# K and Q stored in DRAM by 512 tokens, a planner that counts eight DMAs in flight, and x1 normalised on VectorE and transposed in row halves

## The chip, the cores and the metric

The kernel runs on one core of one Trainium2 chip. The metric is the device time of one execution in microseconds (us); lower is better. A difference of 0.3% (5.6 us) is about what a measurement of this kernel can tell from no change.

## What is computed

Two blocks read the same normalised input and are added to it: attention with 32 heads of 20 columns, and a mixer of shifted tokens with an MLP behind it. S = 2048 tokens, D = 640, F = 1536, everything float32.

```python
xn = layernorm(x)
# A: attention
q, k, v = split(xn @ wqkv)                 # 32 heads, Dh = 20
o = softmax(q k^T * Dh**-0.5) v
A = o @ wo
# B: mixer; it normalises xn once more
h  = gelu(layernorm(xn) @ w1)
hs = shift(h)  # four groups of 160 columns, shifted by +1, -1, +2, -2 tokens
x1 = xn + hs @ w2
B  = x1 + gelu(layernorm(x1) @ w3) @ w4
out = x + A + B
```

## The kernel before, in words

**Work and tiles.** TensorE (PE) has three kinds of products. *Row pairs*: two matmuls with 64 or fewer rows each lie in the two row halves of the array and run at the same time. All dense products are row pairs (every operand is split into a high and a low part, three products each; `twins`, L737), and so are the attention's two products per step: `s` (scores, keys on the partitions, for the exponential on ScalarE, ACT) and `pm` (scores once more, queries on the partitions, from which VectorE, DVE, takes row maxima `mx` for a later block). *Column groups*: four products with 32 columns each, for `pv` (probabilities by values). *Full products*: 128 by 128, the transposes. `SWITCH` (L79) tells the planner that a change of kind costs time.

The attention is a chain of 1024 units in 32 blocks (a block is a pair of heads and 1024 queries). The dense work is spread among the units as filling: the V, Q and K products, w1, the x1 stage (w2), w3, w4; the output product (wo) follows the attention. One stage matters below, the x1 stage (`w23_phase`, L1085): it comes in two halves of four pairs of 128-token tiles, each half followed by the w3 products. For pair q, `x1_pair` (L1121) makes `ps2` on PE, adds the input on DVE (x1), takes bn_stats and a reciprocal root (`rsqrt`, L672: one power on GpSimd, called POOL, and small steps on DVE), and normalises both tiles of 640 columns in place (L1141 to 1143): planned for POOL at 900 ns each, with a way out to DVE at 430 ns. `z_pair` (L1146) then transposes the two tiles on PE (`tz`, ten full 128 by 128 transposes in three PSUM tiles) and `split_held` (L706) moves each PSUM tile out: a copy on ACT, the low part by a subtraction on DVE.

**What sets the order.** Nothing is issued as the program text stands. All operations go into a planner (`Plan.schedule`, L398), which runs a list schedule with a cost for each and writes the instructions of each engine in the order that comes out. On PE a string of some 7,000 letters, `ORDER` (L98), says at each step which kind of group is next (d dense, m maxima, s scores, p values). The hardware runs each engine's instructions strictly in that order: one that waits holds up all behind it on its engine.

**DMAs in the planner.** All DMAs are issued from SyncE (SP), in planned order. Each costs SP 465 ns; its transfer takes nbytes / 260 ns on one common bus; its data are taken to be there 1500 ns later, plus an allowance `late` by kind: `SLOW` 4500 (weights and dense loads), `PREP` 6500 (raw weight chunks `ph_*`, split and written back as `wd_*` for later), `LATE` 7000 (the chain that ends a block), 0 for Q, K and V of the attention.

**The chain that ends a block** (`block_end`, L1478): the sums in `ob` go to DRAM (`od`), come back as `sm` on 128 partitions, DVE takes the reciprocal `rc`, which goes to DRAM (`rcd`) and comes back broadcast as `rb`; POOL multiplies, and the result goes to `onm`. Four DMAs, one after the other, 30 times.

**K and Q.** They lie in DRAM as `[128, 2, 2048]` (row, high or low part, token), L659 and 660; the products write 512 tokens of both parts at a time, the attention reads rows of one part: 2048 tokens of K, 1024 of Q.

Of the kernel before, what the change touches and what calls it, by code (L numbers as in the profile page):

```python
# [52 lines left out]
XB = 12  # L53
BOOT = 740.0
SLOW = 4500.0
PREP = 6500.0
# [31 lines left out]
LATE = 7000.0  # L88
# [15 lines left out]
    "dsdddsdssddsdsddmdmppppsdddsdssdsddsddsddsdddsdssddddsddsdspssdppsddsdsddddssdpsddsdddsddsdsddssddsddddsddsssd"
    "dsppssdddsppsdsdsdssdsddsdspssspppsdsdsdsddssddsddsddsdsdddssddddssdsddsdddssppsdsdddsdspsspsssppsdsdddsddsdpp"
    "dddssdddsdddssdddddsdddsdsddddsdddddsdddssdddddssddddssdddsddddddssdddddsdppppssdddddssddddddsddddsssddddsdddd"
    "dsdsddsddsdppppsddsdsdddddsdsddddsddssddsddddsdsddddsdsdddspssspppsddsdddsddsdddsdsddddssdddddssdddddssddddsds"
    "ppppdsdsdsddsdddsddddsddddssddsdddsddddddddsdsdddddddssddddsdddddssppppsdddssdsdddsddddsddddddsdddsdddsddsdddd"
    "dsssddddsdddsddsddddsppppddsddsddssdsdddsdsddsddddsssdddsdddssddddssdddsddsppppssddsddsddsdsddsddssddsdsddppss"
    "ddddsdsdddsdsddsdsddsdsdpssspppssddddsdsddsdsppssddsddsdddsssdddsdddssdddssddsdsdddsspssspppsdsdddsddddsdsdsdd"  # L110
    "sdddssdsdddssppppsdsdsdsdddsdsdsdsdddsddddssdsdddsddspppdsddsdsddspssddsddsdsddsdsdsddsdsddssdsppppdsdsdsdddds"
    "dssddsdsddddssdddsdssdddddsddsdsdddssppppsddsdsdsddssdddsdsdsdddsdssddsdsddsdsdpssdddsddsdddssppsddsdsdpppsddd"
    "sdsddsddsdsdddssdddsdsdddsddspdsddssdddsssdppppsdsddddsdddsspssdddsdsdsddssdddsdsdsdddssddspssppsspsdsdssdddss"
    "dppssddddddsdsdddsdsddddssdddsdsdddsdsdddsddsddsppsdddssddddsdssddddsdsdsdsppppdsdsdsddsddsddssdddssddddsdsddd"
    "sdssddsppppdssddsdddsddssddsddsdsdsdsdddsdsddssddspsspsdsdddddssppddsddsddsdsddssdsddssppppsdssddsddsddsdsdsdd"
    "ssddppssddddsdspdssdddsdsddsdsddsdspsddsdsddsdssddddsdssddsddddsddsppppssddsdsdsdddsddsddssddsddsdsdsdsddsddds"
    "dddpsddsddspppdsdsddssdsdddddssdsspsdsppsspsdsdsdsddsdddsdsdsddsddsdddsddsdsddsdsppppddsdddssddsddddssdsddsdsd"
    "ddsdssdddssppsssppssddddddssddddddsdsddssdddsddssddsdsddsdsdddsdsppppsdsddssddsddsdsdsddsdsddsdspsspppssdddssd"
    "dsdddsdsdsdsdddsddsddsdddsdsdsdspdpppsddssddddsssdddsddsddsddssddsddspssddpppdsdsddsddssdsddddssddddssdsdddssd"
    "dsddsddddssddsdpsspppsddsdddddsdsddsdddssddssdsddsddsdspsspsdsdddsdsdddsdspsspssspssspssspssspdssspssspssspsds"  # L120
    "psdsddsddsddddsdddsddssdddddddssddddddsddddddssddddddsddsdppppsddssdddsdsdddddsddsdddddddsddddddddsddddssdddsd"
    "dddddsddddsddsppppdddddddddddddddsddddsddddddssddddsddddddddsdddssppddsddsdddsddsdddddsdspdsddddsdddsddddssddd"
    "dsddddddddddppdsddsddddsddsddddsddsdsddsdddsddsppssdddddsdddddddsdddsdddddddsspssdddddsdsdddsdsdsddddssppssspp"
    "ssdddsdsddddsddddsddsdsdsddsdsddddddsdsddsddssddssdppddsspsdddspsssddddddddddddssppssdsssppsssdddsddddddsddddd"
    "dsssddddsddddsssdddddddddddssddddsddsdsdsdsddpppppsddsdddsddsdddsdsdddddsdddsddddsdddsdsdddssdddddsdddddssdddd"
    "dsddddsddsddpppddsdsddddssdddsdsddssdddssddsdddssdppppsdsddssdddssddsdsddsdsddsdsppppdssdddssddsddsdsdsddsdsds"
    "ddspppssddddsdsdddsdddsdsdddssdddsddsddsdddsdsddddssppppssddddddsdddddsdddsdspsdsdsdsdddsdsdsdsddsdsdddsspsssp"
    "ppsdsddsdsdsdsddddssddsdddssddsdsdddssppppdssdddsdsdsdddsddsddsdddsddssdsdddssddsdsppppssddsdsddsddsdsdsddsdds"
    "ddddsdsddddsddssddddsddpppdsdddsddsddsddsddsdsddspsddssdddsdsdsdsddsdsddsddsppssppsdsddsdsdsdsddddssdsddddsspp"
    "ppdsddsddssdddsdsddsdddddsssddddsdsddsdddssdsddddssppssppsssssspssspssspssspsddsddssdddsdddddsdddssddddsddsdsd"  # L130
    "ddsdddsddsppppsdsddddsdddsddsdddddssddsddsddddsdsddsdddddddsdsddspspppdssdddsddsddddssddddsdsddddsddsddddsdddd"
    "ddddddsddddddsdddsddsddddsddddddsdsddddddsddppppsddssdddddsdsddddddsdssddddsddddssdddsdddsdsddddddddddpppsdsdd"
    "dddsddsddddsdddsdsddsdddsdddsddsdddddddsdddddsdspppppsdddssdddssdddddssddddsdsddsdddddddpsdsddddsdddsddsdddddd"
    "ssdddddsdddsddsdddsddspssddddddsspsspsssppssspssspsssspssddddsddddddspssspssspssssspssspssddddsddddsdddsddddss"
    "dddsdddddsdsddddsdddddddddsdsdddsdddsdpppdddsdddddsddddsdsdddddddddsddsdddddddssdddsddddddssddddddsdpppddddddd"
    "dddddddsssdddsdddsddssddsddsdddssppppdsdsdsdddssdsdddsddsdddsssdddsddsdsddsdsdddssdddsppsssppssdddsdsddsdsddss"
    "ddsdsddsdspppssdddsdsddsdsddsddsddsddsppppdsddsdddddsdddsdsdddsdspssdddssddsdsddsdsddsdsddsdsppppssddsddsdddsd"
    "sdsddsddsddssdsddsdsddsdddsdsdsdddsdsppppssdddsdsddsdsddsdsdsdsddsdsppsdsdddsdsdddsdsddsdsdddsdddddssdppppdsdd"
    "ddsdsdddsdsppssdddsdsdsdsdddssddsdddssddddsddsdddsdssddsddsddsppppsdsddsddsdsdsddsdsdsdddsdddsdsddsdsppppsdsds"
    "ddsddssdddssddsddsdsddsddssdddsddsdspsssppsspsssspsdpssspsddsddddspsdsdddssddddsddsddddsdddsdsdddsddsddsdddsds"  # L140
    "dppppsdsdddddsdddddsdddddsddsddddddsssddddddddddddddsddsddsdddsddddddsdddsddssdddddsdddddsddddsddppppsdsddddsd"
    "sdddsddddsddddsdddsdddssdddsdsdddsddsddddsppppdsdddssdddsdddsdsddsddddddsdddddsddsdddsdsdddddsdsppdppsdsdddsdd"
    "sddddssdddsddddssdddsddsddddsddsddsddddsddsppppsddsddsdddsddddsdddssdsdddddsdddsdsddsdddsdddddssddppppdsdsddds"
    "sddddsddddsddssddddddsdsdddsdsddsddddsdddssdppppdsddssddsddddsddsddsddsdddddsdddsddssdddddsddsddddssppppdssddd"
    "dssdddddsdddsdsdsddddsdddsdddsddsddsddsddsddsddppppsdsddddssdddsdddsddsddddsddsdddsdsddsddsddddsddsdsddppppsds"
    "dddddsddsdsdddsdsddsdddsddddsddsdsddddsddsdddsddsppppssdddddssdddsdsdddsddsddddsdddsddddsdsdddsdddsddddssdpppp"
    "sdsddsdddsdddsddsddsddsdddsdsdddddsdsddsdddsddsdddsdsppppssddddssddddsdsddddsdsdddddsdddsddssddddsdsdddsddddss"
    "ppppsddsddsddsddsdsdddsdddddsddsdddssdddsddddssdddsdddsdsppppsddsdsddddsddssddddsdddsddddsdsddsddddssppppdsdss"
    "ddddddddsssddddddsdddssdddddsdddddssdsddddddsdsddsdddsdsdddsppppssddddddssddsddddsdsddddsddsddsddddsdddddsddsd"
    "dddssppppsddsdsdsddddsdddsdddsdddsdsdddsddsdddsddsddsddsddddssppppsddsdsddddssdddddssdddsdddsdddddsddsdsdsdddp"  # L150
    "pppsdddsddddsssddddddsdddssdddddsdsddddddsdddsddsdsdddsdsdddsddsppppssdddsdsddddsddddsdsdsddddsddsdddsdddsddds"
    "dsddsddddssppppsddsddsddsdsdddsdddddsddsddddssddddssdddsdddsdddddssppppsdddsdsdddsddddsdddssdddsdddsdddsdsdddd"
    "dssppppdsdsddddddsssdddddsdddsdsdddsddddddssddddsdsddsddddsdsddsdddsdppppssddddsdddsdsdsdddddsddsdddsdddsdsddd"
    "sdsddsdddsddsddsppppsdddsdsddsddddsddsddsdsdddddsddssddddddssddsddddddssppppdsdsddsddddsdsddddsddssdddsddddsds"
    "dddddsspdpppdssdddddddsssddddddddsdssddddsddddssddddddsdsdsddsdddsdddddsdsppppssddddsddsdddsdsddsddddsdddsddsd"
# [118 lines left out]
class Plan:  # L274
# [123 lines left out]
    def schedule(self):  # L398
# [1198 lines left out]
```

## Time and profile before

| what | value |
|---|---|
| median of 3 runs | 1866.05 us (1861.46 to 1866.73) |
| the profiled execution's own time | 1867.61 us |
| its span, first to last instruction | 1865.7 us |
| PE, DVE, ACT, POOL busy | 1844.3, 1510.3, 1380.1, 478.0 us |
| mean granted TensorE clock | 0.995 |
| bytes moved by DMA | 257.79 MB |

The profile counts an engine as busy while any of its instructions runs. Matmuls overlap (the next one starts before the last has drained), so a busy PE may still have lost time between two starts; that is read from the starts in the timeline. PEld is the loading of weights. Of an instruction's idle time the tables name what ended it.

### The profile page before, as it was taken

To read this page: it belongs to the slowest core of one execution; us is meant where nothing else is said; L and a number is where in the kernel's file an instruction comes from. 1 tells how busy PE (TensorE), PEld (TensorE's weight loads), DVE (VectorE), ACT (ScalarE), POOL (GpSimd) and SP (SyncE) were. 2 spreads that over 40 slices of the span, in tenths; PEclk is the share of its full clock that TensorE was granted. 3 is DMA by queue.
4 is the path that set the end of the run, shared out by engine and by line. 5 is a ranking of instruction groups with operands and counts; after the bars stand their busy time and mean duration, and the time that the engine had idled before them with its cause. 6 is when DMAs were issued, how large, how long until landed. Compare 5 with 4: busy or idle time off the path is not lost.

```text
span 1865.7 us, 44172 instructions
## 1 busy us (share of the span) xinstructions
PE 1844.3 (99%) x17073; PEld 1277.5 (68%) x17073; DVE 1510.3 (81%) x2678; ACT 1380.1 (74%) x2528; POOL 478.0 (26%) x684
## 2 busy tenths in 40 slices
PE   9999999999999999999999999999999999999998
PEld 7876776666666656576666756665777777775687
DVE  8988788898988898877879997778788778788624
ACT  5268778887888886677887676878777777778762
POOL 6011113423413224412113421111211222212211
PEclk9999999999999999999999999999999999999999
DMA  5644646445464575545335574455524243243503
GB/s 196 169 132 152 154 105 175 134 130 171 120 154 126 159 225 152 165 135 168 111 114 181 179 205 143 140 156 176 132 74 108 85 108 93 69 140 97 168 17 114
DMA packets 230361, 257.79 MB, mean 138 GB/s; under 512 B 60520, under 2 KB 175672, under 8 KB 228352
## 3 DMA queue, kind: packets, MB, share of 16 engines
q1 hardware_dynamic: 230152, 254.98, 46.9%
q8 instruction: 134, 2.20, 0.5%
q14 instruction: 75, 0.61, 0.1%
HBM read 151.64 MB, written 103.25 MB: 137 GB/s over the span
## 4 chain that ended last, share of the span: by engine, by line
PE 92%; DVE 3%; POOL 2%; DMA 2%; ACT 1%; issue 0%; DVEq 0%; SPq 0%; POOLq 0%; ACTq 0%
PE ps L355 26%; PE pv L355 24%; PE s L355 14%; PE pm L355 13%; PE psv L355 4%; PE pso L355 3%; PE ps_q L355 3%; PE ps_k L355 3%; DVE mx L323 2%; PE psl L355 1%; POOL x L323 1%; PE tz L323 1%; DMA kpack<-kd 0%; DMA ph_wo<-in_A_wo_dram 0%; PE pmt L355 0%
## 5 line engine op out<-in xcount | busy, mean ns | idle before, releaser
L323 DVE TENSOR_REDUCE mx<-pm 128x1 f32<-128x512 f32 x2048 | 1272.9, 682 | 207.2 <-PE pm L355 128.8
L323 ACT ACTIVATE p<-s 128x512 f32<-128x512 f32 x2048 | 1104.1, 605 | 205.7 <-PE s L355 79.9
L355 PE MATMUL s<-zq,kpack 62*128 62x512 f32 x2048 | 753.7, 408 | 3.5 <-DVE mx L323 3.2
L355 PE MATMUL pm<-kpack,zq 60*128 60x512 f32 x2048 | 752.9, 408 | 0.8 <-DVE mT L323 0.3
L355 PE MATMUL pv<-p,v 128*32 128x512 f32 x4096 | 488.1, 600 | 0.1
L355 PEld LDWEIGHTS s<-zq,kpack 62*128 62x128 f32 x2048 | 360.7, 185 | 109.9 <-issue 33.4
L355 PEld LDWEIGHTS pm<-kpack,zq 60*128 60x128 f32 x2048 | 361.9, 185 | 97.6 <-DVE mx L323 25.6
L355 PE MATMUL ps<-xT,w_w 64*128 64x512 f32 x2040 | 327.5, 393 | 0.1
L355 PEld LDWEIGHTS pv<-p,v 128*32 128x32 f32 x4096 | 116.9, 109 | 236.6 <-issue 209.2
L355 PEld LDWEIGHTS ps<-xT,w_w 64*128 64x128 f32 x2040 | 210.3, 186 | 36.5 <-issue 6.3
L323 POOL TENSOR_TENSOR ob<-ob,obq 128x512 f32<-128x512 f32 x96 | 124.0, 1292 | 365.7 <-ACT obq L323 321.0
L355 PE MATMUL ps<-xT 64*128 64x320 f32 x1632 | 170.8, 308 | 0.0
L355 PEld LDWEIGHTS ps<-xT 64*128 64x128 f32 x1632 | 146.1, 186 | 15.1 <-issue 5.0
L323 ACT COPY obq<-pv 128x512 f32<-128x512 f32 x84 | 49.3, 587 | 123.5 <-PE pv L355 123.5
L355 PE MATMUL ps<-xT,gT 64*128 64x320 f32 x1152 | 122.2, 306 | 0.0
L343 POOL MEMSET scratch<- 1x1 f32 x134 | 12.2, 91 | 404.8 <-PE ps L355 235.5
L355 PEld LDWEIGHTS ps<-xT,gT 64*128 64x128 f32 x1152 | 105.8, 186 | 6.9 <-issue 0.8
L355 PE MATMUL psv<-wv,xT 64*128 64x320 f32 x960 | 93.1, 309 | 1.1 <-ACT xT L323 1.1
L355 PEld LDWEIGHTS psv<-wv,xT 64*128 64x128 f32 x960 | 81.6, 185 | 8.1 <-issue 2.2
L355 PE MATMUL ps_q<-xT,w_q 64*128 64x512 f32 x480 | 81.8, 395 | 0.2 <-POOL scratch L343 0.2
L355 PE MATMUL ps_k<-xT,w_k 64*128 64x512 f32 x480 | 78.0, 398 | 0.0
L355 PE MATMUL pso<-wos,oT 64*128 64x320 f32 x768 | 67.2, 307 | 0.0
(184 smaller groups left out, 1411.3 us busy)
## 6 DMA issues: line engine op xcount, KB each, us to landing
zq<-qd SPq DMA_DIRECT2D x156, 80.0 KB
kpack<-kd SPq DMA_DIRECT2D x78, 160.0 KB
w_w<-wd_w SPq DMA_DIRECT2D x48, 256.0 KB
gd<-pre SPq DMA_DIRECT2D x8, 1536.0 KB
g<-gd SPq DMA_DIRECT2D x64, 192.0 KB
wd_w<-ph_w SPq DMA_DIRECT2D x34, 320.0 KB
xT<-wd_w SPq DMA_DIRECT2D x34, 320.0 KB
vd<-vst SPq DMA_DIRECT2D x32, 256.0 KB
```

The lines of the kernel that those rows point to most:

```text
L323: o.insts = [getattr(e, m)(val(out), *[val(x) for x in ins], **{k: val(v) for k, v in kw.items()})]
L343: o.insts = [nc.gpsimd.memset(scratch.get(), 0.0)]
L355: o.insts = [nc.tensor.matmul(out.get(), lhsT.get(), rhs.get(), **kw) for out, lhsT, rhs, kw in products]
```

## The change

- `qd` and `kd` become `[128, 4, 2, 512]`: 512 tokens of both parts lie together. A product writes one run of 4096 bytes per row in place of two of 2048; the attention reads runs of 2048 bytes (four per row of K, two of Q) in place of one of 8192 and one of 4096.
- The planner's DMA: SP's cost, and a transfer time worked out from the number of runs and their length over 16 engines; at most eight DMAs in flight; data after 1600 ns plus an allowance that is now 2500 (`SLOW`), 3000 (`PREP`), 3000 (`LATE`), and 1500 for Q and K.
- x1 is normalised on DVE alone.
- `tz` is made of 64-row halves: each 128 by 128 transpose becomes a row pair of two transposes, one per half of the tokens, into two PSUM tiles of up to 512 columns; per pair of tiles there are two rounds (four column tiles, then one), so four PSUM tiles and four copies and subtractions in place of three.
- Two DVE costs in the planner are raised (455 for the addition of 320 columns), and `ORDER` is another string.

```diff
+LANES = 8
-SLOW = 4500.0
-PREP = 6500.0
+SLOW = 2500.0
+PREP = 3000.0
-LATE = 7000.0
+LATE = 3000.0
 ORDER = (
-    "dddddddddddddmddddmdddddddddddddddddddddddddddddmdmdddddddddddddddddddmddddddmddddmdddddddddddddddddddmddddd"
...
+        lanes = [0.0] * LANES
...
             if e == "dma":
                 xbus = max(xbus, o.end) + o.xfer
-                o.end = xbus + 1500.0 + o.late
-                free[e] = max(free[e], xbus - BACKLOG)
+                lanes.append(xbus + 1600.0)
+                o.end = xbus + 1600.0 + o.late
+                free[e] = max(free[e], lanes[-LANES] + 70.0)
...
-    def dma(o, i, nbytes, **kw):
-        op_ = pl("dma", 465.0, "dma_start", o, i, xfer=nbytes / 260.0, **kw)
+    def dma(o, i, nbytes, es=2560, **kw):
+        n = nbytes / es
+        op_ = pl("dma", 375.0 + 100.0 * (n >= 128) + 130.0 * (n >= 256), "dma_start", o, i,
+                 xfer=1.1 * (8.0 + 0.0375 * es) * math.ceil(n / 16), **kw)
...
-    qd = [dt([P, 2, S], F32R, f"qd{c}") for c in range(ND)]
-    kd = [dt([P, 2, S], F32R, f"kd{c}") for c in range(ND)]
+    qd = [dt([P, 4, 2, 512], F32R, f"qd{c}") for c in range(ND)]
+    kd = [dt([P, 4, 2, 512], F32R, f"kd{c}") for c in range(ND)]
...
-                kept[nm, tb] = dma(_f(dst[:, :, tb * 512:(tb + 1) * 512]), _f(hl), 524288)
+                kept[nm, tb] = dma(_f(dst[:, tb]), _f(hl), 524288, 4096)
...
                 for j in range(2):
-                    pl("pool", 900.0, "tensor_scalar", x1[:, j, :], x1[:, j, :], mv[:, j, 0:1], rs[:, j:j + 1],
-                       op0=ALU.subtract, op1=ALU.mult, port=True, alt=("dve", 430.0, "tensor_scalar", True))
+                    pl("dve", 430.0, "tensor_scalar", x1[:, j, :], x1[:, j, :], mv[:, j, 0:1], rs[:, j:j + 1],
+                       op0=ALU.subtract, op1=ALU.mult, port=True)
...
-                for d0 in (0, 2, 4):
-                    n = min(2, ND - d0)
-                    ps = pd(f"tz{q}_{d0}")
+                for d0, n in ((0, 4), (4, 1)):
+                    pss = [pd(f"tz{q}_{d0}_{h}")[:, :P * n] for h in range(2)]
                     for e in range(n):
                         for j in range(2):
-                            transpose(ps[:, e * 256 + j * P:e * 256 + (j + 1) * P], x1[:, j, (d0 + e) * P:(d0 + e + 1) * P])
-                    split_held(xT[:, 0, d0:d0 + n, t0:t0 + 256], xT[:, 1, d0:d0 + n, t0:t0 + 256],
-                             ps[:, :256 * n].rearrange("p (d t) -> p d t", d=n), 256 * n)
+                            c = e * P + j * 64
+                            pl.group("row", 110.0, [(pss[h][:, c:c + 64], x1[64 * h:64 * h + 64, j, (d0 + e) * P:(d0 + e + 1) * P],
+                                                     ident[64 * h:64 * h + 64, 64 * h:64 * h + 64], dict(is_transpose=True))
+                                                    for h in range(2)])
+                            tick(110.0)
...
     def rdma(o, i, nbytes):
-        adma(o, i, nbytes)
+        adma(o, i, nbytes, 1500.0)
```

**PE, before, at the second pair of x1 tiles** (`tz` of the pair with x1 tile 1; `x_1` is the normalised tile, `ps_4` the sums of the next pair):

```order
5508 L355 MATMUL ps_4_1_11831<-xT 128x320
5509 L355 MATMUL ps_4_0_11830<-xT 128x320
5510 L355 MATMUL pm_0_12017<-kpack_76,zq_79 128x512
5511 L355 MATMUL s_1_12018<-zq_80,kpack_77 128x512
5512 L323 MATMUL tz_0_12025<-ident,x_1_11124 128x128 x4
5513 L323 MATMUL tz_2_12032<-ident,x_1_11124 128x128 x4
5514 L323 MATMUL tz_4_12040<-ident,x_1_11124 128x128 x2
5515 L355 MATMUL pv_2_11811<-p_0_11650,v_8708 32x512
```

The ten transposes stand in one piece, between row pairs and a column group. After the change the same pair's transposes begin like this:

```order
5610 L356 MATMUL ps_5_1_12178<-xT 128x320
5611 L356 MATMUL ps_5_0_12177<-xT 128x320
5612 L356 MATMUL s_0_12329<-zq_80,kpack_77 128x512
5613 L356 MATMUL pm_1_12330<-kpack_76,zq_79 128x512
5614 L356 MATMUL pm_0_12333<-kpack_76,zq_79 128x512
5615 L356 MATMUL s_1_12334<-zq_80,kpack_77 128x512
5616 L356 MATMUL tz_0_0_12341<-ident,x_1_11219 128x64
5617 L356 MATMUL tz_0_1_12342<-ident,x_1_11219 128x64
5618 L356 MATMUL tz_0_0_12341<-ident,x_1_11219 128x64
```

They are row pairs among row pairs, and they have moved back behind sums of the pair after next (`ps_5`, where `ps_4` stood).

**DVE, after, at the fourth pair** (`x1_3`), from the addition of its last sums (`ps2_7`) to its normalisation; `mx13` are the attention's maxima, `xT` the low parts of the pair before:

```order
1213 L324 TENSOR_REDUCE mx13_11025<-pm443_1_12831 128x1
1214 L324 SCALAR_TENSOR_TENSOR rv_c3_12097<-mv3_3_12141 128x2
1215 L324 TENSOR_TENSOR xT_201<-tz2_0_1_12823,xT_201 128x4x2x64
1216 L324 TENSOR_REDUCE mx13_11025<-pm443_0_12844 128x1
1217 L324 SCALAR_TENSOR_TENSOR rt_c3_12113<-ry_c3_12142 128x2
1218 L324 TENSOR_REDUCE mx13_11025<-pm444_1_12881 128x1
1219 L324 SCALAR_TENSOR_TENSOR rt_c3_12113<-rt_c3_12113,rv_c3_12097 128x2
1220 L324 TENSOR_TENSOR xT_201<-tz2_4_0_12892,xT_201 128x2x64
1221 L324 SCALAR_TENSOR_TENSOR ry_c3_12142<-rt_c3_12113,ry_c3_12142 128x2
1222 L324 TENSOR_REDUCE mx13_11025<-pm444_0_12900 128x1
1223 L324 TENSOR_TENSOR xT_201<-tz2_4_1_12893,xT_201 128x2x64
1224 L324 TENSOR_SCALAR x1_3_12394<-x1_3_12394,mv3_3_12141,ry_c3_12142 128x640 x2
```

The two normalisations (row 1224) are now in DVE's own line; ahead of these rows stand the two additions, one maximum, two bn_stats, a subtraction and bn_aggr (rows 1207 to 1212).

**SP, the start of a block's closing chain, before** (block 11: `od` out, `sm` back; `rd`, `xr`, `ph` and `xT` are loads and stores of the dense work):

```order
490 L323 DMA od_123<-ob11_11158 4x512
491 L323 DMA rd_117<-xr5_12060 128x640
492 L323 DMA ph_w3_9_1_12311<-in_B_w3_dram 128x2x128
493 L323 DMA xT_201<-hsd2_114 128x2x256
494 L323 DMA xT_201<-hsd3_115 128x2x256
495 L323 DMA xT_201<-hsd4_116 128x2x256
496 L323 DMA rd_117<-xr6_12212 128x640
497 L323 DMA xr7_12526<-in_A_x_dram 128x640
498 L323 DMA sm11_10738<-od_123 128x16
```

And after:

```order
531 L324 DMA od_123<-ob11_11058 4x512
532 L324 DMA wd_w4_8_1_318<-ph_w4_8_1_12193 128x640
533 L324 DMA ph_w4_9_0_12283<-in_B_w4_dram 128x320
534 L324 DMA xr7_12594<-in_A_x_dram 128x640
535 L324 DMA sm11_10789<-od_123 128x16
```

`sm`, which waits for `od`, has moved from the eighth to the fourth DMA behind it.

More of the change, by code (lines that the diff above doesn't have):

```diff
@@ L104 @@
[L104 to L113, printed above, removed]
@@ L774, in prep @@
         w = dt([P, 2, n], F32R, "wd_" + name)
-        dma(_f(w), _f(hl[:, :, :n]), n * 1024).late = PREP
+        dma(_f(w), _f(hl[:, :, :n]), n * 1024, 8 * n if n == 320 else 4 * n).late = PREP
         wdone[name] = w
@@ L959, in tile_kernel @@
     pl("dve", 198.0, "tensor_copy", r2t, ps[:NT, :P])
-    dma(r2d, r2t, 8192)
+    dma(r2d, r2t, 8192, 512)
     gate = [pl.ops[-1]]
@@ L1133, in x1_pair @@
                         c0, c1 = 320 * n, 320 * (n + 1)
-                        pl("dve", c_dve(320), "scalar_tensor_tensor", x1[:, j, c0:c1], xr[:, c0:c1], lnk[:, 0, ti:ti + 1],
+                        pl("dve", 455.0, "scalar_tensor_tensor", x1[:, j, c0:c1], xr[:, c0:c1], lnk[:, 0, ti:ti + 1],
                            ps, op0=ALU.mult, op1=ALU.add, dk=K_FE)
@@ L1195, in w3_tile @@
                     pl("act", c_act(GB * S // 2, False), "activation", pv, pv, AF.Gelu_apprx_tanh, table="gelu")
-                    dma(gd[f // GB][:, :, half * 1024:(half + 1) * 1024], pre, 2097152)
+                    dma(gd[f // GB][:, :, half * 1024:(half + 1) * 1024], pre, 524288 * GB, 4096)
             ahead([f"w3_{f}" for f in range(NF)], lambda n: early(wcol, sp, n), w3_tile)
@@ L1248, in w4_phase @@
             for n, ps in enumerate(pss):
-                pl("dve", c_dve(320), "scalar_tensor_tensor", r[:, n, :], r[:, n, :], lnk[:, 1, t:t + 1], ps,
+                pl("dve", 455.0, "scalar_tensor_tensor", r[:, n, :], r[:, n, :], lnk[:, 1, t:t + 1], ps,
                    op0=ALU.add, op1=ALU.add, dk=K_FE)
@@ L1263, in load_o @@
             pl("pool", 600.0, "memset", oc[64:], 0.0, port=True)
-        dma(oc[:m], onm[k * P:k * P + m, b * 512:(b + 1) * 512], m * 2048).late = 2000.0
+        dma(oc[:m], onm[k * P:k * P + m, b * 512:(b + 1) * 512], m * 2048, 2048).late = 2000.0
         return oc
@@ L1357, in tile_kernel, with adma @@
     fill["on"] = False
-    def adma(o, i, nbytes, late=0.0):
+    def adma(o, i, nbytes, late=0.0, es=2048):
         k = pl.key
         pl.key = k + K_DMA
-        r = dma(o, i, nbytes)
+        r = dma(o, i, nbytes, es)
         r.late = late
@@ L1390, in load_k @@
                         b = 64 * e + slot * DH + o
-                        rdma(_f(t[b:b + n, s]), _f(src[r0:r0 + n, part, s]), n * (s.stop - s.start) * 4)
+                        rdma(_f(t[b:b + n, s]).rearrange("p (c t) -> p c t", c=4), _f(src[r0:r0 + n, :, part, :]), n * S * 4)
     def load_q(blk):
@@ L1402, in load_q @@
                     b = 64 * e + slot * DH + o
-                    rdma(_f(t[b:b + n, :]), _f(src[r0:r0 + n, part, sl]), n * HALF * 4)
+                    rdma(_f(t[b:b + n, :]).rearrange("p (c t) -> p c t", c=2),
+                         _f(src[r0:r0 + n, qh * 2:qh * 2 + 2, part, :]), n * HALF * 4)
     vt, mx, pvs = {}, {}, {}
```

156 lines of the change are left out of this document (84 added, 72 removed).

## The prediction

> **What bounds the kernel now.** First the page's totals and its chain of waits:
>
> ```profile
> span 1865.7 us, 44172 instructions
> PE 1844.3 (99%) x17073; PEld 1277.5 (68%) x17073; DVE 1510.3 (81%) x2678; ACT 1380.1 (74%) x2528; POOL 478.0 (26%) x684
> PE 92%; DVE 3%; POOL 2%; DMA 2%; ACT 1%; issue 0%; DVEq 0%; SPq 0%; POOLq 0%; ACTq 0%
> ```
>
> PE is the bound: 92% of the chain that ended last is its own work, and it is idle for 21.4 us of the span. Only three things can shorten the kernel: fewer idle gaps on PE, a full clock, less work on PE. So next come PE's waits (columns: total us, times, longest):
>
> ```profile
> PE tz L323 <- POOL x L323: 6.9, 6, 2.2
> PE s L355 <- DVE mx L323: 3.2, 2, 2.2
> PE psv L355 <- ACT xT L323: 1.1, 1, 1.1
> PE ps L355 <- POOL scratch L343: 1.1, 2, 0.9
> ```
>
> A third of the idle time is one cause: transposes of x1 that wait for POOL's normalisation. No row names a DMA. PE's timeline shows two of the places, the second and fourth pair of x1 tiles, and the group row of POOL says why:
>
> ```profile
> 730.93 0.33 PE L323 MATMUL tz<-ident,x 128*128 128x128 f32 x1 [0.30 <-POOL x L323]
> 733.42 2.18 PE L323 MATMUL tz<-ident,x 128*128 128x128 f32 x9 [2.16 <-POOL x L323]
> ...
> 783.81 2.12 PE L323 MATMUL tz<-ident,x 128*128 128x128 f32 x9 [2.16 <-POOL x L323]
> L323 POOL TENSOR_SCALAR x<-x,mv,ry_c 128x640 f32<-128x640 f32 x12 | 30.5, 2550 | 10.4 <-DVE ry_c L323 10.4
> L323 DVE TENSOR_SCALAR x<-x,mv,ry_c 128x640 f32<-128x640 f32 x4 | 2.5, 659 | 0.0
> ```
>
> One tile takes POOL 2550 ns, where the planner counts 900; the first transpose starts after one tile, the next waits for the other. DVE does the same tile in 659 ns. Last the stretches around these places and two others (us; busy us of PE, PEld, DVE, ACT, POOL; granted clock; DMA share; GB/s):
>
> ```profile
> 420.00:430.00 10.00, 9.31 (x63) 6.67 (x65) 8.41 (x15) 6.78 (x13) 4.33 (x7) 0.83 0.72 178
> 732.70:739.60 6.90, 6.18 (x29) 2.88 (x31) 2.51 (x5) 2.03 (x4) 3.44 (x3) 0.51 0.24 88
> 783.90:787.40 3.50, 3.50 (x17) 2.33 (x21) 1.93 (x4) 2.15 (x5) 1.88 (x5) 0.51 0.00 1
> 980.00:990.00 10.00, 9.79 (x54) 3.55 (x57) 7.71 (x13) 8.72 (x18) 0.97 (x1) 0.83 0.88 245
> 697.00:785.00 88.00, 83.18 (x775) 57.22 (x772) 75.25 (x155) 57.61 (x111) 42.56 (x40) 0.96 0.53 157
> 1024.00:1107.00 83.00, 80.79 (x741) 50.14 (x740) 77.95 (x155) 60.93 (x119) 34.87 (x38) 1.00 0.68 202
> ```
>
> Behind both waits PE runs at half clock, for 6.9 and 3.5 us (windows cut to the whole lapse). The last two rows are the two x1 stretches, four pairs each.
>
> **The change part by part.** *Normalisation on DVE, tz later.* The 6.9 us of waits go, and the half clock behind two of them: (6.9 + 3.4) / 2 = 5.1 us. Both rest on the new order holding x1 ready. DVE gets 12 x 0.659 = 7.9 us, seven tiles in the first stretch and five in the second. The rows for its steps, and for what PE's cover is made of:
>
> ```profile
> L323 DVE TENSOR_REDUCE mx<-pm 128x1 f32<-128x512 f32 x2048 | 1272.9, 682 | 207.2 <-PE pm L355 128.8 <-PE s L355 70.0 <-PE psv L355 0.3
> L323 DVE SCALAR_TENSOR_TENSOR x<-xr,lnk,ps 128x320 f32<-128x320 f32 x32 | 15.9, 539 | 0.0
> L323 DVE BATCH_NORM_STATS2 bn_c<-x 128x6 f32<-128x320 f32 x32 | 14.4, 481 | 0.0
> L323 DVE BATCH_NORM_AGGREGATE mv<-bn_c 128x2 f32<-128x12 f32 x16 | 3.2, 198 | 0.1
> L323 DVE TENSOR_TENSOR xT<-tz,xT 128x512 fp32r<-128x512 f32 x16 | 10.6, 685 | 7.9 <-ACT xT L323 7.9
> L323 DVE SCALAR_TENSOR_TENSOR rv_c<-mv 128x2 f32<-128x2 f32 x8 | 1.7, 210 | 0.1
> 904.57 0.39 PE L355 MATMUL s<-zq,kpack 62*128 62x512 f32 x1
> 904.89 3.64 PE L355 MATMUL pv<-p,v 128*32 128x512 f32 x32
> 910.40 0.39 PE L355 MATMUL pm<-kpack,zq 60*128 60x512 f32 x1
> 910.40 0.39 PE L355 MATMUL s<-zq,kpack 62*128 62x512 f32 x1
> 910.63 0.39 PE L355 MATMUL ps<-xT,w_w 64*128 64x512 f32 x2
> 1023.25 0.40 PE L355 MATMUL s<-zq,kpack 62*128 62x512 f32 x1
> 1023.57 1.31 PE L323 MATMUL tz<-ident,x 128*128 128x128 f32 x10
> 1024.82 0.49 PE L355 MATMUL s<-zq,kpack 62*128 62x512 f32 x1
> ```
>
> From starts: a row pair of 512 columns takes 910.63 - 910.40 = 0.23 us, and its two halves start together; a row pair followed by another kind takes 904.89 - 904.57 = 0.32, so a switch of kind costs 0.09; 32 matmuls of pv take about 3.42 us (3.64 less the tail), 0.855 per column group; ten transposes 1.25 less a switch, 0.11 to 0.12 each.
>
> Is x1 ready in the new order? For pair 3, the fourth (counted from 0), DVE's rows as the section above shows them, from the additions to the first normalised tile: two additions 1.08, five maxima 3.41, two bn_stats 0.96, subtractions of two 512-column tiles 1.37 and of two 128-column ones some 0.6 (an estimate: under half of 0.685), bn_aggr 0.2, four small steps at up to 0.21 some 0.8, the tile 0.66: 9.1 us. PE has, between that pair's last sums and its first transpose, ten row pairs of transposes (1.1), eight of 512 columns (1.84), four column groups (3.42), four switches (0.36): 6.7. PE would wait 2.4 us, or 0.6 if both additions and one maximum lie ahead of the point I count from; I take the middle, 1.5. Counted likewise, pair 7 is late by 0.4 (bounds -0.4 and 1.3), the other six have 17 to 25 us of cover for 5 to 10 us of DVE and wait for nothing. Together +1.9. A half clock behind pair 3 (a lapse of 3.4 us costs 1.7) I give half a chance: +0.9. DVE's 1.3 us in one piece puts off the maxima queued behind it, which `s` and `ps` wait for at block ends; the only such waits now are 3.2 us, and I add a quarter: +0.8 (bounds 0 and 3.2).
>
> *Transposes as row pairs.* PE's switches of kind go from 476 to 442 by the two orders: 34 x 0.09 = -3.1. 80 transposes of 0.11 become 80 pairs of halves. No row shows a 64-column one; the nearest are the transpose, of which a half has half the columns (0.055), and a row pair of 320 columns:
>
> ```profile
> 1025.15 1.04 PE L355 MATMUL ps<-xT,hs 64*128 64x320 f32 x12
> 1026.03 0.39 PE L355 MATMUL pm<-kpack,zq 60*128 60x512 f32 x1
> ```
>
> Six pairs take 0.88, so 0.147 each. The pair then costs between 0.055 and 0.147, against 0.11: -4.4 to +3 us. I take 0, the transpose's own row being nearest: same data, same 128-column stationary operand. Four copies and subtractions for three per pair of tiles cost ACT and DVE about 0.2 us per pair, 1.6 in all, beside PE.
>
> *K and Q, planner's DMAs.* The same bytes in more, shorter runs. PE waits for no DMA, so nothing can be gained on that side but order (0); what can be lost is the slack. The planner's allowance for a closing chain falls from 1500 + 7000 to 1600 + 3000 ns: 3.9 us less room. Who would wait is DVE, in its reciprocal:
>
> ```profile
> L323 DVE RECIPROCAL rc<-sm 128x16 f32<-128x16 f32 x30 | 7.3, 242 | 0.0
> ```
>
> Idle time before it was 0.0 in 30 blocks; with maxima queued behind it, a late `sm` would reach PE. I take 0, as the shown SP rows also put `sm` four places nearer to `od`; upper bound under the rivals.
>
> *POOL* loses 30.5 us: it is busy for 26%, and nothing on the path but the waits already counted follows from it.
>
> *Sum*, against the profiled execution of 1867.6: -6.9 - 5.1 - 3.1 + 1.9 + 0.9 + 0.8 = -11.5, so 1856.1. The median of the runs is 1.6 lower than the profiled execution, so 1854.5. A second way agrees: DVE's work in the first stretch becomes 75.25 + 7 x 0.66 + 0.8 = 80.7 of 88 us, in the second 77.95 + 5 x 0.66 + 0.8 = 82.1 of 83. Filled without a gap DVE lets these stretches shorten by 7.3 and 0.9; with the switches, -11.3.
>
> [...] The rows show half clock after gaps of 2.2 us. [...]
>
> **The rivals.** *Whole order better.* The order is searched anew, so the other waits shown (3.2 + 1.1 + 1.1) and half clock at 420 and 980 (3.4) may go too: for it, nothing ties them to x1; against it, 81% busy DVE has to take more. With 5.4 + 3.4 and the 0.9 not paid: 1844.8. *DVE becomes the bound in the x1 stretches.* At 80.7 of 88 and 82.1 of 83 us it has little room, and its queue is in order: the 6.9 us of waits come back as waits for `mx`, half of the clock loss too. 1867.6 - 3.1 - 2.6 - 1.6 = 1860.3. Against it: PE has 17 to 25 us of cover at six pairs. *The lapses have another cause.* For: the row 980:990 has clock 0.83 with PE busy 9.79 of 10. The lapses stay: 1854.5 + 5.1 - 0.9 = 1858.7. [...] *The halves don't run together.* Then each pair costs two times 0.11: 80 x 0.11 = +8.8, 1863.3. Against it: `s` and `pm` at 910.40 do. *Slower: closing chains come late.* The allowance is cut by 3.9 us, runs are shorter and more of them, and DVE's `rc` waits for `sm` in each of 30 blocks, maxima behind it. If each such wait puts PE back by one maximum, 0.68 us, that is +20.5: 1875.0. It decides (slower than 1871.6) from (1871.6 - 1854.5) / 30 = 0.57 us per block. Against it: idle 0.0 in that row, and half the DMA engines' time is free in the first stretch (0.53).
>
> **How the numbers follow.** 0.3% (5.6 us) is about what a measurement can tell from no change, so faster means under 1860.5, slower over 1871.6. Forecast 1854.5: 0.42, with its own range 1847 to 1861 (the transposes' -4.4 and +3, pair 3's and DVE's bounds). Whole order better 0.15, DVE bound 0.14 (half of it faster, half same), other cause of the lapses 0.08, halves apart 0.06, late chains 0.15. Faster: 0.42 + 0.15 + 0.07 + 0.08 less 0.04 of the forecast's upper edge = 0.68; same: 0.07 + 0.06 + 0.04 = 0.17; slower 0.15. The range runs from 1841 (somewhat below the whole order's 1844.8, for its own uncertainty) to 1867, which leaves out the late chains and little else.
>
> **What would show it right or wrong.** Right: no row of PE's waits names POOL `x`; `tz` waits only at the fourth pair, for DVE `x`, under 2.4 us; granted clock 1.00 in the first x1 stretch but for one lapse at most; halves of `tz` starting together, ten pairs in about 1.1 us. Wrong: `rc` with idle time before it, or PE waits on `mx` above 4 us (chains, DVE); full clock missing where there is no gap (another cause); `tz` halves one behind the other; a DMA among PE's releasers.

## The result, and the profile after

The changed kernel takes 1880.11 us (median of 6 runs, 1878.34 to 1883.95), the kernel before 1865.39 us beside it: ratio 1.0086, 95% interval 1.0071 to 1.0100. It is 0.9% slower, 15 us, where 0.6% faster was forecast. The profiled execution took 1878.9 us.

The page's totals and chain of waits, after:

```profile
span 1876.7 us, 44340 instructions
PE 1841.3 (98%) x17153; PEld 1286.3 (69%) x17153; DVE 1517.7 (81%) x2696; ACT 1389.4 (74%) x2545; POOL 446.9 (24%) x665
PE 85%; DMA 6%; DVE 5%; ACT 1%; SPq 1%; POOL 1%; issue 1%; DVEq 0%; ACTq 0%; POOLq 0%
```

PE is busy for 3 us less than before, and idle for 35.4 us (1876.7 - 1841.3) where it was 21.4. In the chain DMA has grown from 2% to 6%. PE's waits (total us, times, longest):

```profile
PE s L356 <- ACT p L324: 4.9, 2, 4.7
PE pm L356 <- ACT p L324: 4.5, 3, 3.9
PE s L356 <- DVE mx L324: 3.5, 2, 3.0
PE pm L356 <- DVE mx L324: 2.7, 3, 1.3
PE s L356 <- DMA zq<-md: 2.1, 2, 1.9
...
PE tz L356 <- DVE mx L324: 1.6, 1, 1.6
```

The row `tz <- POOL x` (6.9 us before) is gone. In its place stand waits for `p`, the exponentials on ACT, and `mx`, the maxima on DVE. Both are ends of a queue: an instruction ahead of them on ACT or DVE was itself waiting. The groups show for what (last column: idle time before the group, and what ended it):

```profile
L324 ACT CAST ph_w<-ph_w 128x320 fp32r<-128x320 f32 (+2 forms) x60 | 25.2, 422 | 21.4 <-DMA ph_w<-in_B_w_dram 20.2 <-issue 1.1
L324 DVE RECIPROCAL rc<-sm 128x16 f32<-128x16 f32 x30 | 7.3, 244 | 11.8 <-DMA sm<-od 11.8
```

ACT waits 20.2 us for raw weight chunks (`ph_w`, first the load, then the copy that makes the high part), and DVE's reciprocal, with no idle time ahead of it before, waits 11.8 us for `sm`. One such wait from end to end, at 770 us: SyncE's timeline, then ACT's, then PE's.

```profile
755.56 3.45 SPq L324 DMA_DIRECT2D zq<-qd  x6
759.62 6.46 SPq L324 DMA_DIRECT2D kpack<-kd  x6
...
769.09 0.33 SPq L324 DMA_DIRECT2D ph_w<-in_B_w_dram  x1
```

```profile
767.05 1.11 ACT L324 ACTIVATE p<-s 128x512 f32<-128x512 f32 x2 [0.39 <-PE s L356]
775.37 0.46 ACT L324 CAST ph_w<-ph_w 128x320 fp32r<-128x320 f32 x1 [7.21 <-DMA ph_w<-in_B_w_dram]
775.73 2.56 ACT L324 ACTIVATE p<-s 128x512 f32<-128x512 f32 x5
```

```profile
776.38 0.80 PE L356 MATMUL s<-zq,kpack 62*128 62x512 f32 x2 [4.67 <-ACT p L324]
```

ACT stands at the split from 768.2 us, before SyncE has even issued its load (769.09, behind six reads of K that took 6.5 us to issue). The data are there at 775.3; five exponentials are queued behind the split, and PE stops for 4.67 us. In the kernel before, the same kind of place reads like this (SyncE, then ACT):

```profile
750.16 2.36 SPq L323 DMA_DIRECT2D kpack<-kd  x6
...
754.04 0.43 SPq L323 DMA_DIRECT2D ph_w<-in_B_w_dram  x1
...
757.33 0.38 SPq L323 DMA_DIRECT2D ph_w<-in_B_w_dram  x1
```

```profile
765.66 0.44 ACT L323 CAST ph_w<-ph_w 128x256 fp32r<-128x256 f32 x1
767.70 0.40 ACT L323 CAST ph_w<-ph_w 128x256 fp32r<-128x256 f32 x1
```

The splits stand 11.6 and 10.4 us behind their loads and wait for nothing. Six reads of K were issued in 2.4 us there. The same thing on DVE, after, at 667 us: `rc` waits, and five maxima behind it, and PE for 3.00 us (DVE's timeline, then PE's):

```profile
666.85 0.25 DVE L324 RECIPROCAL rc<-sm 128x16 f32<-128x16 f32 x1 [3.75 <-DMA sm<-od]
667.02 3.01 DVE L324 TENSOR_REDUCE mx<-pm 128x1 f32<-128x512 f32 x5
```

```profile
667.70 0.49 PE L356 MATMUL s<-zq,kpack 62*128 62x512 f32 x1 [3.00 <-DVE mx L324]
```

The stops are not the whole price. At each of the four places where PE stops for 3 us or more (330, 440, 667 and 771 us, the first in two pieces) the clock falls to half (granted clock 0.58 over 667.7 to 671.8 us); the other three stretches (us; busy us of PE, PEld, DVE, ACT, POOL; granted clock; DMA share; GB/s):

```profile
330.00:340.00 10.00, 8.30 (x47) 6.28 (x49) 7.96 (x14) 8.81 (x16) 3.44 (x4) 0.66 0.68 178
440.00:450.00 10.00, 6.06 (x34) 2.69 (x36) 3.94 (x8) 3.79 (x8) 2.41 (x3) 0.66 0.31 85
770.00:780.00 10.00, 5.33 (x26) 1.70 (x26) 3.85 (x8) 3.34 (x7) 1.20 (x2) 0.71 0.66 231
```

The mean granted clock was 0.990 to 0.995 in the six runs of the changed kernel, 0.992 in the mean. In the runs of the kernel before that stand beside the experiments below it was 0.995 to 0.999, 0.997 in the mean. 0.005 of 1870 us is 9 us of clock; as a part of the half clock falls into the stops themselves (from 443.1 us on in the stop that ends at 444.7), that is an upper estimate of its share in the 15 us.

### The profile page after: what moved, and what is told of

Read it like the earlier page. It is cut to its first block, busy times and chain, and to the rows that moved or that the text cites. A ratio compares the mean times of both kernels' runs of the same rounds, so it can differ in the third digit from the quotient of the medians.

```text
span 1876.7 us, 44340 instructions
## 1 busy us (share of the span) xinstructions
PE 1841.3 (98%) x17153; PEld 1286.3 (69%) x17153; DVE 1517.7 (81%) x2696; ACT 1389.4 (74%) x2545; POOL 446.9 (24%) x665
## 4 chain that ended last, share of the span: by engine, by line
PE 85%; DMA 6%; DVE 5%; ACT 1%; SPq 1%; POOL 1%; issue 1%; DVEq 0%; ACTq 0%; POOLq 0%
PE ps L356 24%; PE pv L356 22%; PE s L356 13%; PE pm L356 12%; PE psv L356 3%; PE pso L356 3%; PE ps_k L356 3%; PE ps_q L356 3%; DVE mx L324 3%; DMA ph_w<-in_B_w_dram 2%; SPq L324 1%; PE psl L356 1%; DMA kpack<-kd 1%; DMA sm<-od 1%; ACT p L324 1%
## 5 line engine op out<-in xcount | busy, mean ns | idle before, releaser
L356 PEld LDWEIGHTS pv<-p,v 128*32 128x32 f32 x4096 | 120.8, 110 | 231.3 <-issue 198.6
```

The lines of the kernel that those rows point to most:

```text
L356: o.insts = [nc.tensor.matmul(out.get(), lhsT.get(), rhs.get(), **kw) for out, lhsT, rhs, kw in products]
```

## The experiments

Theory 1: the cut allowances let ACT and DVE come to splits and reciprocals before their data, and what is queued behind them holds up TensorE. Theory 2: the new order of TensorE, or the x1 edits in it, is what is slow. Theory 3, formed on the way: any change of the planner's numbers under a kept order string spoils its fit. Ratios are against the kernel before, measured beside each run on the same chip, so runs are best compared with each other by their ratios. In the runs of the first and the third group every instruction of TensorE keeps its place.

### Order kept: later splits, old rows of K and Q

**Splits 4 us later.** After the planning, the list is sorted again with the splits' start times raised by 4 us:

```diff
+        pl.soft.update((o, 4000.0) for o in pl.ops[i0:])   # copy, subtraction, store of a raw chunk
```

> The kernel after, every instruction of TensorE, and all else, in the same order, but each split of a raw weight chunk (ph: the copy on ACT or DVE, the subtraction, the store) stands 4 us later in the planned order. Theory 1 (ACT waits in order for raw chunks that the planner takes to be there too early, and the exponentials behind it hold up TensorE): the four waits of ACT that reach TensorE (at 330, 440, 550 and 770 us) go, TensorE idles 10 to 13 us less, and the time is 1866 to 1870 us. Theory 2 (the new order or the x1 edit is what is slow, the waits of ACT only name it): 1878 to 1882 us as after.

1877.04 us, ratio 1.0082 (1.0058 to 1.0105), by the ratio no better than the after (1.0086). ACT's waits on `ph_w` fell from 20.2 to 1.0 us as meant, but `rc` still waits 11.5 us, PE now waits on `w_w <- wd_w` for 1.0 us (weights whose chunks were stored later), and the wait at 667 us has become two.

**And reciprocals 3.5 us later**

```diff
-        pl("dve", 185.0, "reciprocal", rc, sm)
+        pl.soft[pl("dve", 185.0, "reciprocal", rc, sm)] = 3500.0
```

> As the run with splits 4 us later, and besides the 30 reciprocals of the closing chains (rc, which wait for sm) 3.5 us later in the order. Theory 1 says that rc's waits (11.8 us in 4 pieces, one of which held TensorE for 3.1 us at 667 us) go too: 1863 to 1866 us. Theory 2: no change against after, 1878 to 1882 us. If only the splits matter, the same as the run before it within 2 us.

1878.2 us, 1.0084 (1.0069 to 1.0099): nothing more. `rc` now waits 0.5 us, but POOL waits 53.2 us for `rb`, which comes out of the same chain (27.4 in the after), and PE 2.4 us for weights and 1.8 for `T`. An instruction put off is not data come earlier: everything that hangs on it is late by as much. By their numbers both runs speak for theory 2; they don't refute theory 1, because they took the wait away in a way that made others.

**K and Q by whole rows, in the after** (one line of the edit; `qd`, the writes and the reads change with it)

```diff
-    kd = [dt([P, 4, 2, 512], F32R, f"kd{c}") for c in range(ND)]
+    kd = [dt([P, 2, S], F32R, f"kd{c}") for c in range(ND)]
```

> The kernel after with K and Q in DRAM as before (one run of 2048 or 1024 tokens per row), every engine's order unchanged. Theory 1a (the shorter runs of K make SyncE slow: 742 ns per K read where it took 329, six in a row, so what is issued behind is 2.5 us late and meets the cut allowances): half or more of the late raw chunks come in time, 1869 to 1875 us. Theory 1b (the cut allowances alone do it): 1878 to 1882 us.

1880.71 us, 1.0093 (1.0076 to 1.0109): no gain, with K and Q in whole rows again. ACT still waits 16.4 us on `ph_w`.

**K and Q by 512 tokens, in the before** (the reverse edit)

> The kernel before with K and Q in DRAM by 512 tokens, every engine's order as before. SyncE loses 0.4 us per K read here too, but the old allowances (6.5 us for raw chunks, 7 us for the closing chain) leave room: if the allowance is what decides, 1865 to 1867 us, no wait of ACT on ph. If the shorter runs alone do harm, 1870 us or more.

1861.99 us, 0.9998 (0.9987 to 1.0008): the layout alone costs nothing where the plan has room. This run also says something of the clock. Its order is that of the kernel before, and so is its wait at 733 us; PE's timeline, and the window around it (us; busy us of PE, PEld, DVE, ACT, POOL; granted clock; DMA share; GB/s):

```profile
733.11 1.20 PE L323 MATMUL tz<-ident,x 128*128 128x128 f32 x9 [2.17 <-POOL x L323]
```

```profile
730.00:740.00 10.00, 7.54 (x69) 4.93 (x69) 7.38 (x15) 5.88 (x13) 7.10 (x7) 1.00 0.25 77
```

The same gap, and a clock of 1.00 where the kernel before had 0.66. One execution doesn't settle it: the control further down has the same order, and there the half clock is back.

### Parts of the change, and the order string

**Allowances cut, in the before**

```diff
-SLOW = 4500.0
-PREP = 6500.0
-LATE = 7000.0
+SLOW = 2500.0
+PREP = 3000.0
+LATE = 3000.0
```

> The kernel before with only the three allowances of the planner cut (SLOW 2500, PREP 3000, LATE 3000), its order string kept: TensorE's order stays but for some 30 instructions of 14,951, ACT's and SyncE's orders move (splits and reciprocals stand earlier behind their loads). Theory 1 (cut allowances put splits and reciprocals on ACT and DVE before their data are there): ACT waits on ph_w and DVE on sm appear as in the after (10 us and more each), time 1874 to 1884 us. Theory 2 (the allowances do no harm by themselves; the order or the x1 edit does): 1862 to 1868 us.

1879.3 us, 1.0087 (1.0067 to 1.0108): as much as the whole change loses, with only these three numbers cut. The waits are mostly not where theory 1 put them, though: `rc` waits 2.4 us, ACT 2.3 on `ph_k`; PE stops for 3.2 us behind a DVE that stands at a split of `ph_q` (219 us), and for 3.2 us at a `scratch` of POOL (743 us). A `scratch` is a one-element write on POOL that waits for one group of TensorE and is waited for by a later one; this one stood in POOL's queue behind two x1 tiles that took 4.99 us together.

**Old allowances, in the after** (the reverse edit)

> The kernel after with the three old allowances (SLOW 4500, PREP 6500, LATE 7000), the rest and the order string as after: TensorE's order stays but for some 20 instructions. Theory 1: ACT's waits on ph_w and DVE's on sm go, TensorE's waits at 330, 440, 667 and 776 us with them, 1858 to 1866 us. Theory 2: 1876 to 1882 us. In between if data come later than even the old allowances, or other loads (not splits and chains) are pushed back: 1868 to 1875 us.

1886.61 us, 1.0120 (1.0100 to 1.0140): slower still, against theory 1's number. ACT's waits on `ph_w` fall to 5.0 us and `rc`'s go, but PE waits 4.5 us for the first w3 weights and 2.6 at a `scratch` of POOL.

**Allowances raised, in the before** (SLOW 6500, PREP 9000, LATE 10000)

> The kernel before with the three allowances raised instead of cut (SLOW 6500, PREP 9000, LATE 10000): as many instructions move as in the run with cut allowances. Theory 1 (too little allowance lets in-order engines wait for data): more allowance does no harm, 1860 to 1868 us. Theory 3 (the order string is fitted to one set of numbers, and any other set, larger or smaller, spoils the fit): 1872 to 1884 us, as with the cut ones.

1925.75 us, 1.0346 (1.0332 to 1.0361). This is theory 3, and more than it said: PE waits 10.3 us for `xT <- wd_w` and 10.2 for `wv <- wd_v`, weights whose preparation the plan now puts late. In these three runs the kept string, with other numbers than those it was searched with, sends PE to groups whose data are not there. So they can't price the allowances.

**The new string alone, in the before**

> The kernel before with the new order string alone (4,156 lines of TensorE's order differ). If the new string is good by itself (fewer switches of kind, more cover before the transposes): 1855 to 1863 us, and no long wait for POOL's x. If a string is good only with the planner numbers and the operations that it was searched with: 1870 us or more.

1899.42 us, 1.0201 (1.0187 to 1.0215): the same lesson.

**x1 on DVE alone, in the before** (TensorE's order does not move)

```diff
-                    pl("pool", 900.0, "tensor_scalar", x1[:, j, :], ..., alt=("dve", 430.0, "tensor_scalar", True))
+                    pl("dve", 430.0, "tensor_scalar", x1[:, j, :], ...)
```

> The kernel before with x1 normalised on DVE alone, TensorE's order unchanged, whole transposes. The waits for POOL's x and the half clock behind them go, some 2 us come back as waits for DVE's x or maxima: 1854 to 1860 us. If DVE is the bound there: 1862 to 1866 us. Against the run with both x1 edits it shows the row halves' share, 3 to 4 us by their measured length.

1857.4 us, 0.9969 (0.9953 to 0.9985): faster by 6 us. PE's waits no longer name POOL `x`, and the first x1 stretch, at a clock of 0.96 in the kernel before, runs at 1.00 (same columns as above):

```profile
697.00:785.00 88.00, 85.78 (x810) 57.95 (x809) 84.66 (x174) 60.88 (x119) 27.52 (x39) 1.00 0.59 172
```

**Both x1 edits, in the before**

> The kernel before with the two x1 edits alone (normalised on DVE, transposed in row halves), planner and order string as before. By the prediction's terms: TensorE's waits for POOL's x (6.9 us) and the half clock behind them (5.1 us) go, pairs of halves measured at 0.065 us in the after save 4 us, DVE gives some back: 1851 to 1857 us. If DVE is the bound in the x1 stretches: 1859 to 1864 us.

1872.94 us, 1.0050 (1.0035 to 1.0065): 15.5 us above the run with DVE alone, and far from the 1851 to 1857 expected. Some of that may again be the string, since other instructions of TensorE moved with the transposes; how much isn't shown. Some is the halves' own: the fifth pair's second round waits until DVE has emptied a PSUM tile of the first (PE's timeline):

```profile
1032.38 0.27 PE L355 MATMUL tz<-ident,x 64*128 64x64 f32 x1
1033.76 0.33 PE L355 MATMUL tz<-ident,x 64*128 64x64 f32 x3 [1.11 <-DVE xT L323]
```

**Whole transposes, in the after** (the reverse edit)

> The kernel after with whole 128 by 128 transposes (three PSUM tiles per pair, as before), the rest and the order string as after. On the old order the row halves cost 15.5 us (1872.9 against 1857.4) although TensorE's own time for them is 4 us less. Theory H (two PSUM tiles held at once and four subtractions on a nearly full DVE cost more than the shorter matmuls save, in any order): 1868 to 1877 us. If the new order had made room for them: 1882 to 1890 us.

1892.22 us, 1.0166 (1.0152 to 1.0180): theory H's number is missed, and the other is the nearer one; taking the halves away from the string that was searched with them costs 0.8%, 15 us. What they are worth in an order of their own stays open: the two comparisons disagree in sign, and both moved TensorE's order.

### Waits taken away, every order and every DMA kept

These kernels leave the weights unsplit, and from the second on the attention's sums unused; only their times count.

**Splits of a constant** (`high` is the chunk's high part)

```diff
+        pl.swap[pl.ops[i0]] = high, (same,)                 # copy: same is a constant tile
+        pl.swap[pl.ops[i0 + 1]] = high, (same, _f(high))    # subtraction
```

> The kernel after, every engine's order and every DMA kept, but each split of a raw weight chunk reads a constant tile in place of the chunk (copy and subtraction work on the constant and write the high part alone; the products use wrong weights), so that ACT, DVE and POOL never wait for a raw chunk. Theory 1: ACT's 31 us of waits on ph go, and TensorE's waits behind them (at 330, 445 and 776 us): 1866 to 1871 us. Theory 2 (the new order of TensorE is slower by itself): 1877 to 1881 us.

1866.66 us, 1.0021 (1.0009 to 1.0032). Against the after's 1.0086 that is 0.65%, 12 us, for nothing but ACT, DVE and POOL not waiting for raw chunks. PE's waits:

```profile
PE s L358 <- DVE mx L326: 3.1, 2, 2.9
PE s L358 <- DMA zq<-md: 2.4, 1, 2.4
PE ps L358 <- DMA w_w<-wd_w: 2.1, 1, 2.1
PE tz L358 <- DVE mx L326: 1.6, 1, 1.6
```

The rows with `ACT p` are gone; the 2.9 us on `mx` is the reciprocal's wait.

**And reciprocals of a constant**

```diff
-        pl("dve", 185.0, "reciprocal", rc, sm)
+        pl.swap[pl("dve", 185.0, "reciprocal", rc, sm)] = rc, (onesm[:, :n],)
```

> As the run with splits of a constant, and the reciprocal of each closing chain reads a constant too in place of sm (the normalisation is wrong), so that DVE never waits for sm. Theory 1: the wait at 667 us goes too, and with it what the waits shifted: 1858 to 1866 us, that is the before or below. Theory 2: 1877 to 1881 us.

1861.15 us, 0.9990 (0.9977 to 1.0004): another 0.31%, 6 us. On ACT and DVE no split and no `rc` waits for a load, and the kernel is as fast as the before. What is left of late data now stands on PE itself:

```profile
PE s L358 <- DMA zq<-md: 3.5, 2, 3.3
PE ps L358 <- DMA w_w<-wd_w: 3.2, 1, 3.2
PE pm L358 <- DVE mx L326: 2.1, 2, 1.9
PE tz L358 <- DVE mx L326: 1.6, 1, 1.6
```

**Control: the same edit in the before**

> Control: the kernel before with splits and reciprocals of a constant (same things left out). Its ACT and DVE waited 0 us on ph_w and sm, so nothing can be gained: 1862 to 1866 us under either theory. Anything below says that the edit saves time in another way, and that much is to be taken off the gain of the two runs before it.

1862.36 us, 0.9989 (0.9978 to 1.0000): 0.1% at most is the edit's own. This decides between the theories: the new order of TensorE, left exactly as it is, runs as fast as the old one once the engines don't wait for loads.

The control also keeps the gaps of 2.2 us for POOL's x, at 732 and 783 us, and has half clock at both, as the kernel before had (same columns as above):

```profile
730.00:740.00 10.00, 7.84 (x46) 4.25 (x48) 4.75 (x11) 3.35 (x7) 5.21 (x3) 0.66 0.24 76
780.00:790.00 10.00, 7.68 (x44) 4.08 (x42) 6.10 (x14) 5.57 (x13) 5.23 (x8) 0.83 0.29 88
```

**And old rows of K and Q**

> The kernel after with splits and reciprocals of a constant, and K and Q in DRAM as before (SyncE 329 ns per K read for 742). If SyncE's slower K reads delay other loads (weights, g, V) that TensorE waits for, 3 us or more below the run without old rows; if those loads are late for other reasons, the same within 2 us.

1857.97 us, 0.9975 (0.9962 to 0.9987): 0.15% (3 us) below the run without the old rows; the two intervals overlap, so SyncE's slower K reads are shown as a cost here only weakly. PE's waits for weights are no longer among its first rows, and `zq <- md` is down from 3.5 to 2.8 us:

```profile
PE s L358 <- DMA zq<-md: 2.8, 3, 1.2
PE pm L358 <- ACT p L326: 2.2, 3, 1.5
PE tz L358 <- DVE mx L326: 1.6, 1, 1.6
```

### The version that beats both

**x1 on DVE, and K and Q by 512 tokens**, in the before; planner, string and transposes as they were.

> The two parts of the change that cost nothing on the old order: x1 normalised on DVE, and K and Q by 512 tokens; planner, order string and transposes as before. The terms add up if they are independent: 1857.4 from the run with DVE alone, and 0 to -1.5 from the layout: 1855 to 1858 us. If the later K reads on SyncE now meet a fuller DVE: 1860 us or more.

1857.73 us, 0.9975 (0.9965 to 0.9985), 5 us faster than the before and 1.1% faster than the after. Its interval lies within that of the run with DVE alone, so no gain of the layout is seen; DVE alone is the whole gain, and the simpler version.

## Why the prediction was wrong

**The step that failed** is "K and Q, planner's DMAs": "I take 0, as the shown SP rows also put `sm` four places nearer to `od`". One place in the order was read for 30 chains and 109 raw chunks (70 of them `ph_w`). The term measured 12 us (splits) plus 6 us (reciprocals), the stops and the half clock that comes with them together. That step also looked for who would wait in one place only: "Who would wait is DVE, in its reciprocal". The larger payer was ACT, in the splits of raw chunks, whose allowance (`PREP`) was cut just as much and which has the exponentials queued behind it. Every instruction that takes a weight, a raw chunk or a chain's data stood under the cut numbers, and each of them should have been listed with what is queued behind it.

**The same step left out SyncE.** "The same bytes in more, shorter runs" was costed for the transfer, not for the issue. Six reads of K took 2.36 us to issue; with the new rows they take 4.85 in the old order and 6.46 at 760 us of the after, and what stands behind them is later by that; the new planner counts a read of K as 375 ns. By itself this costs nothing (0.9998 in the before). Where the allowance is gone it is worth some 3 us at most, shown only weakly: in the after itself the old rows gained nothing (1.0093).

**The rival that came true** is the slower one, "closing chains come late": its sign held, and its cause (3.9 us less room) for a third of the loss, 6 of 18 us. That its sum came near (1875.0 against 1880.1) is luck, since its mechanism was mis-drawn: not one maximum, 0.68 us, in each of 30 blocks, but a few long stops (4.7, 3.9 and 3.0 us at PE), most of them not at a closing chain. Its 0.15 was too low. The argument held against it, "idle 0.0 in that row", was a fact of the old allowances, the very thing that the change took away; and "half the DMA engines' time is free" speaks of bandwidth, where what counts is when a load is issued and how long one takes at worst (at 771 us: issued at 769.09, there at 775.3).

**Held:** the waits for POOL's x are gone, in the after and in every run with x1 on DVE. The fourth pair's transposes wait 1.6 us, forecast 1.5 (0.6 to 2.4); that is partly luck, as the pair's two tiles took DVE 2.65 us there, where the working has 0.66 for one. DVE's other steps are as long as taken (in the after an addition 0.54 us, a bn_stats 0.48), and DVE didn't become the bound: with 84.66 of 88 us in the first stretch, the run with DVE alone gained 6 us.

**Mis-sized:** that run's part of the sum was -6.9 - 5.1 + 1.9 + 0.9 + 0.8 = -8.4; it measured -6.0. The clock terms are not what fell short. The mean granted clock was 0.9990 in the five runs with DVE alone and 0.9968 in the eight runs of the kernel before beside them; 0.0022 of 1860 us is 4.1 us (an estimate), and the sum had -5.1 + 0.9 = -4.2. The lapses stand at the two gaps in two of the three traces with the gaps (the kernel before and the control; not the run with K and Q by 512 tokens), and there is none in the trace without them. In the kernel before one lapse begins at 732.7 us, inside the gap that ends at 733.4, the other at 783.9, 0.1 us behind its gap. So the rival "the lapses have another cause" is not borne out for these two places: the lapses come with the gaps, though not in every execution. What is left for the waits is some 2 us where the sum had -6.9 + 1.9 + 0.8 = -4.2; what took the rest isn't shown. The row halves' 0 per pair was too high on PE: eight halves start within 0.28 us (after, PE's timeline), 0.07 per pair against 0.11, some 3 us in all; what they cost on PSUM tiles was not in the sum.

```profile
798.21 0.46 PE L356 MATMUL tz<-ident,x 64*128 64x64 f32 x8 [1.63 <-DVE mx L324]
798.49 0.48 PE L356 MATMUL s<-zq,kpack 62*128 62x512 f32 x1
```

**Open:** how much of the x1 gain survives in the after. With all waits for chunks and sums gone it is 1861.15, where -8.4 from the x1 part and -3.1 from the switches would have it near 1851. Two waits left on PE (`zq <- md` 3.5, first w3 weights 3.2) are 6.7 us of these 10, but no run took both away, and no run shows the 3.1 us of the switches by themselves.

## What to carry to other kernels

A planner's allowance for DMA latency is not slack to be trimmed: on an engine that runs in order, an instruction that waits for a load puts its wait on everything queued behind it (at 771 us a split that waited 7.21 us held five exponentials, and with them PE for 4.67), and the price is set by the latest loads, not the typical one (in the after ACT waited only 7 times for the 70 `ph_w` loads, but up to 7.2 us). When such a number changes, list every instruction that takes a DMA's data, on every engine, with its queue; rows without idle time in the profile of before show only that the old number sufficed. An order that was searched is best taken to belong to the numbers and operations it was searched with (here a kept string under other planner numbers lost 0.3 to 3.5%): judge a single part by an edit that leaves the order alone, or by taking the wait away and leaving the instruction in its place.

## What the runs showed of the hardware

- SyncE took longer to issue the same bytes in more runs: six reads of K of 8192-byte rows took 2.36 us (kernel before, at 750 us), in 2048-byte runs 4.85 us in the same order (at 747 us):

```profile
746.98 4.85 SPq L323 DMA_DIRECT2D kpack<-kd  x6
```

- A gap of 2.2 us on PE came with half clock in two executions of one order (0.66 over 730 to 740 us, in the kernel before and in the control) and with full clock in a third (1.00). In the kernel before another gap of 2.2 us, up to 1225.5 us, came with full clock (1.00 over 1223.4 to 1226.9). The eight lapses within the spans of the traces of before and after lasted 3.413 us (four of them) or 6.827, and within one execution they began whole multiples of 3.413 us apart: in the kernel before at 422.1, 732.7, 783.9 and 981.9 us, which is 91, 15 and 58 times that, in the after at 330.5, 443.1, 668.4 and 774.2 us, 33, 66 and 31 times. Which gaps bring a lapse isn't shown.
- DVE's normalisation of a 128 by 640 tile took 0.6 us in 14 of 16 cases of the after. The other two are the fourth pair's, 2.65 us for both (1.16 and 1.56) where a pair took 1.12 to 1.14 elsewhere, and there POOL had tensor operations running when they began (DVE's timeline, then POOL's):

```profile
794.91 2.65 DVE L324 TENSOR_SCALAR x<-x,mv,ry_c 128x640 f32<-128x640 f32 x2
```

```profile
794.86 0.87 POOL L324 TENSOR_TENSOR ph_w<-ph_w 128x320 fp32r<-128x320 f32 x1 [2.08 <-ACT ph_w L324]
795.68 1.52 POOL L324 TENSOR_TENSOR rb<-ob,rb 128x512 f32<-128x512 f32 x1
```

  Each of the two ended 0.35 us after the POOL operation that was running when it began. In the after's two cases where POOL's operation began after DVE's tile, the tile took 0.61 us. In the run with DVE alone the longest of 16 took 1.84 us, the median 0.60. In the kernel before two of DVE's four tiles began while POOL normalised another, and took 0.80 and 0.61 us. A step that moves from POOL to DVE was slower beside POOL in some of these cases, not in all; what decides isn't shown.
